# Two output tiles of group 0 computed by seven half products instead of four whole ones, and a new order of all operations, in an attention and feed-forward kernel

## The chip, the core and the metric

The kernel runs on one core of a Trainium2 chip. Five engines work side by side, each through its own list of instructions in order, and wait for one another through semaphores: PE (matrix products), DVE and POOL (vector work), ACT (activations) and SP, which here only issues transfers. The metric is the device time of one execution in microseconds (us), as the median of several runs. The profile is one further execution, recorded by the hardware profiler.

## The reference

Attention with a squared ReLU in place of softmax, followed by a feed-forward layer with a quick GELU:

```python
scores = scale * np.matmul(q, k.transpose(0, 1, 3, 2))     # q, k, v: 8 x 12 x 448 x 64
attn = np.maximum(scores, 0.0) ** 2 / S
attn_out = np.matmul(attn, v)
x = np.ascontiguousarray(attn_out.transpose(0, 2, 1, 3)).reshape(B * S, H * D)   # 3584 x 768
h = x @ w_in                                                # 768 x 2048
g = h * (1.0 / (1.0 + np.exp(-1.702 * h)))
return (g @ w_out).astype(np.float32)                       # 2048 x 768
```

## The kernel before

The work is cut into 24 attention units (8 batches, 3 units of four heads each) and 8 groups of tokens, of 6 x 64 = 384 tokens (even groups) and 8 x 64 = 512 tokens (odd groups). A group's feed-forward work can begin when the units of its batches have delivered their columns of the transposed x.

The kernel's whole order is one hand-held list of short words (`words`, from line 468 on). `do(word)` parses each word and issues its operation. So the order of the words is the order of the instructions on every engine, and also the order of the transfers on the queues of SP, POOL and ACT. The part after `@` gives the PSUM banks (0 to 7) that the operation takes; a new tile in a bank waits until the readers of the bank's last tile are done. The part after `:` names the engine (`a` ACT, `d` DVE, `p` POOL) where it isn't the usual one.

The words, with their lines in the profile:

| word | operation | engine |
|---|---|---|
| `Lk6`, `Lq6` | load k or q of unit 6 in float32 into the one staging buffer of k (`kst`) or q (`qst`) | SP's queue (L99) |
| `K6`, `Q6` | cast it to float16, which frees the staging buffer | ACT, POOL or DVE (L79, L83) |
| `Rk6`, `Rq6` | transpose it by a transfer | SP's queue |
| `jk1`, `jq1`, `V1` | load and cast k, q or v in one transfer; units 1 to 5 for k and q | POOL's queue (L104) |
| `tk1`, `ek1` | transpose on PE (L131) and its copy out; units 0 to 5 | PE, DVE |
| `s7.4@6.2` | scores of unit 7, part 4, into two banks | PE (L150) |
| `r7.4.1` | ReLU of one of the two banks | ACT (L163) or DVE (L161) |
| `x7.4` | square of both halves | DVE (L88), ACT (L169), POOL (L88) |
| `a7` | squared scores times v: 28 matmuls | PE (L181) |
| `e7.0.1` | copy of a part of the result into x of a group | ACT, DVE |
| `f0.3.1` | first product of the layer, plain: two matmuls of group 0 or 1 | PE (L228) |
| `u2.1.4` | first product by seven half products: product 4 of group 2, block 1; six matmuls | PE (L203, `hx`) |
| `S`, `T` | sums of w_in blocks and of x blocks that these need | DVE (L88) |
| `t`, `b`, `g`, `v` | snapshot, add, GELU and scaling to float16 of the first product | ACT, DVE, ACT, POOL (L79, L88, L214, L217) |
| `m0.1.0` | second product, plain: tile 1 of group 0, output half 0; 16 matmuls of 384 columns | PE (L203, `op`) |
| `n0.1.0` | its copy to the output tile | ACT, DVE |
| `p1.0.4` | second product of two tiles together by seven half products: product 4 for tiles 0 and 1 of group 1; 8 matmuls of 384 columns | PE (L203, `ox`) |
| `i2.2.1` | second product of one tile with the combined weights; 16 matmuls | PE (L203, `os`) |
| `A1.0.4` | sums of token tiles that `p` and `i` need (`asum` and in place) | DVE (L88) |
| `W2.4` | sums of w_out blocks: quarter 2 of combination 4 | DVE (L88, `wT`) |
| `h`, `l` | snapshot of a pair's bank to the output tile, and the final addition | ACT or DVE, DVE or ACT (L81, L85, L396) |
| `o`, `q` | store of a whole output tile (two transfers), or a half of a half tile | SP's queue; `q` also ACT's |
| `jwa`, `jwb`, `jo` | load of w_in pieces and w_out blocks | POOL's queue (L411, L415) |
| `G3` | a tiny transfer on SP that waits for the last w_in piece | SP's queue |

For two token tiles and the two output halves, four `m` of 16 matmuls are the plain way. The seven products (a Strassen form) take seven `p` of 8 matmuls. They accumulate in two banks, 0 for products 0, 2, 4, 5 and 1 for products 1, 3, 6. Between them the snapshots `h0`, `h2`, `h4` and the additions `l1`, `l3`, `l6` read the banks: product 2 waits for `h0`, 4 for `h2`, 5 for `h4`, 3 for `l1` and 6 for `l3`. Products 2 and 3 need the token sums `A.2` and `A.1` and weight combinations 2 and 1. Products 4 and 5 need `A.3` and combinations 3 and 4, and product 6 needs `A.4`.

Combination 3 overwrites a block of w_out in place:

```python
        o, x, y = {1: (t1, wout[1][0], wout[0][0]), 2: (t2, wout[1][1], t1),
                   3: (wout[1][0], wout[1][0], wout[1][1]), 4: (t4, wout[0][1], t2)}[n]
```

so all plain `m` of output half 1, which read the block as loaded, must come before the four `W.3`. In the kernel before, group 0's three tiles are the plain `m` and `n` (six `m`), and groups 1 to 7 use `p`, with `i` for the odd third tile of groups 2, 4 and 6.

The buffers that matter below: one each for `kst` and `qst`, two for the cast k and q, three for the transposed ones, four for v, five for `gf` (GELU results before scaling) and three output tiles.

Of the kernel before, what the change touches and what calls it, by code (L numbers as in the profile page):

```python
# [15 lines left out]
def kernel(  # L16
# [406 lines left out]
    with tc.manual_schedule():  # L423
# [35 lines left out]
        def zeros(e, p, n):  # L459
# [8 lines left out]
            "Lk0 z13@0 jk1 V1 jq1 I V0 K0:d tk0@1 z1 ek0 jk2 Lq0 Q0:a tq0@2 eq0 tk1@3 s0.3@4.5 "  # L468
            "r0.3.1 jq2 ek1 s0.1@6.7 r0.1.0 r0.3.0:d s0.0@0.1 s0.2@2.3 tq1@5 r0.0.1:d r0.2.0 "
            "s0.5@4.6 r0.1.1 s0.4@1.2 r0.0.0 r0.5.1 s0.6@7.0 eq1 r0.4.0:d tk2@5 x0.0 s1.0@1.6 "  # L470
            "r0.4.1 x0.4 jwb2 r0.5.0 x0.5 r0.6.1 jk3 r0.2.1 r0.6.0 x0.3:p jq3 x0.1 ek2 r1.0.1 "
            "r1.0.0 x0.2 x0.6 s1.5@2.4 s1.2@0.3 r1.2.0 s1.1@7.6 r1.1.1 tq2@5 a0@1.0 r1.1.0 r1.5.0 "
            "s1.6@6.7 eq2 r1.2.1 x1.0 r1.5.1 r1.6.0 s1.3@5.2 r1.3.0 x1.1 x1.2 tk3@3 e0.0.0 "
            "e0.0.1:a jk4 x1.5 e0.1.0:a tq3@4 r1.3.1 ek3 eq3 jwb0 x1.3 jq4 jwa0 s1.4@6.5 r1.6.1 "
            "V2 x1.6 r1.4.1 r1.4.0 s2.0@1.3 s2.2@2.7 r2.2.1 e0.1.1:a s2.1@4.5 r2.0.1 r2.0.0 "
            "r2.2.0 tk4@6 r2.1.1 x1.4 a1@7.0 e1.0.1:a ek4 r2.1.0:d x2.2 s2.6@3.6 r2.6.0 tq4@1 "
            "r2.6.1 e1.0.0 s2.3@2.4 r2.3.0 e1.1.1 x2.0 x2.1 eq4 s2.4@5.0 r2.3.1 jwa1 s2.5@3.6 "
            "f0.2.0@2 r2.4.0 r2.4.1 jwb1 jwa2 jq5 f0.3.0@4 s3.0@1.5 x2.6 e1.1.0 x2.3 f0.3.1 x2.4 "
            "jk5 r2.5.0 r2.5.1 x2.5 r3.0.0:d S0.1 V3 f0.2.1 f0.0.0@7 f0.0.1 s3.1@0.3 r3.0.1 "
# [24 lines left out]
            "b1.3.1 b1.2.3 g1.2.3 Rk7 u1.2.5 u1.2.6 u1.3.4 r6.1.0 W3.1 S0.4 v1.2 V7 u1.3.3 g1.2.5 "
            "v1.2.3 s6.4@4.5 s6.3@6.0 S1.3 n0.0.1 t1.3.4 g1.3.1 b1.2.6 b1.3.3 s6.5@3.7 r6.4.0 "
            "u1.3.5 x6.1:p r6.3.0:d r6.4.1:d r6.5.0 W1.2 v1.3.1 v1.2.5 u1.3.6 Lk8 g1.3.5 W3.2 V6 "
            "x6.4:a r6.3.1:d x6.2:a r6.5.1 Rq8 b1.3.6 K8:p m0.1.0@4 s6.6@6.3 W2.4 v1.3.5 g1.3.3 "
            "v1.3.3 s7.2@5.1 g1.2.6 x6.3 W1.4 v1.2.6 Lq9 g1.3.6 s7.0@0.2 r7.2.1 r7.0.0 x6.5:a Q9 "
            "r6.6.1:d r7.2.0:d Lk9 r7.0.1 m0.1.1@7 r6.6.0:d n0.1.0:a Rk8 s7.1@3.1 x6.6 W3.4 "
            "x7.0:a a6@5.0 s7.3@6.2 r7.1.0:d r7.1.1 n0.1.1 Lq10 s7.4@4.3 x7.2 e6.0.1:a K9:p "  # L510
            "r7.3.1 e6.1.1:a e6.0.0 r7.4.0:d p1.0.0@1 o0.0 r7.4.1:d e6.1.0:a s7.6@7.2 s7.5@0.5 "
            "r7.3.0 x7.1 x7.3 r7.6.0 r7.6.1:d r7.5.0 s8.2@4.6 m0.2.0@3 r7.5.1 r8.2.0:d V10 x7.4 "
            "s8.1@7.0 x7.6 r8.2.1 x7.5:a h1.0.0 n0.2.0:a s8.0@5.6 r8.1.1 a7@2.4 v1.3.6 r8.0.1 "
            "A1.0.1@0 A1.0.2@1 s8.3@3.0 W0.4 r8.3.0 r8.1.0:d e7.0.1 e7.1.1:a r8.3.1 p1.0.1@6 "
            "s8.5@7.3 V8 e7.0.0:a r8.0.0:d x8.1 e7.1.0 r8.5.0:d Rk9 r8.5.1 Rq9 s8.6@4.5 x8.0 x8.2 "
            "r8.6.1 x8.3:a p1.0.2 x8.5 r8.6.0:d s8.4@0.2 r8.4.1 s9.0@3.7 r8.4.0 l1.0.1 r9.0.0 "
            "x8.6 r9.0.1 x8.4 x9.0:a m0.2.1@5 n0.2.1:a s9.1@2.4 A1.0.4 r9.1.1:d Lk10 r9.1.0 "
            "a8@0.3 s9.2@7.5 e8.0.0:a Q10:d e8.0.1:a s9.3@4.2 r9.2.1:d r9.3.1 K10:p p1.0.3 "
            "u2.0.0@5 r9.2.0 Rk10 u2.1.0@2 Lk11 K11:p T2.1 W3.3 e8.1.0 T2.2 T2.3 e8.1.1:a "
            "s9.4@7.3 u2.0.1@0 W1.3 r9.4.1:d t2.0.0 u2.0.2 b2.0.1 t2.1.0 u2.1.2 u2.1.1@3 r9.3.0:d "  # L520
            "b2.1.1 W0.3 T2.4 r9.4.0 t2.0.2 u2.0.3 u2.0.4 g2.0.1 v2.0.1 t2.1.2 u2.2.0@7 g2.1.1 "
            "t2.0.4 b2.0.3 Lq11 t2.2.0 v2.1.1 u2.1.4 t2.1.4 h1.0.2 x9.2 u2.1.3 b2.1.3 u2.2.1@4 "
            "u2.0.6 g2.0.3 v2.0.3 b2.2.1 x9.4:a u2.2.2 u2.1.6 b2.0.6 g2.2.1 g2.0.6 Rq10 W2.3 "
            "u2.2.3 u2.3.0@0 Q11:a b2.1.6 t2.2.2:d u2.0.5 v2.0.6 g2.1.6 u2.3.1@3 g2.1.3 t2.3.0:d "
            "b2.3.1 v2.1.6 v2.2.1 u2.2.4 u2.1.5 u2.3.2 u2.3.3 t2.2.4 u2.2.5 A1.0.3 b2.2.3 u2.2.6 "
            "Lk12 o0.1 g2.3.1 t2.3.2 v2.3.1 v2.1.3 g2.0.5 g2.1.5 v2.0.5 u2.3.4 p1.0.4 g2.2.3 "
            "g2.2.5 s9.6@5.2 v2.1.5 b2.2.6 s9.5@4.7 t2.3.4:d u2.3.5 x9.1:a v2.2.3 K12 Lq12 b2.3.3 "
# [147 lines left out]
```

## Time and profile before

| what | value |
|---|---|
| median of 10 runs | 369.87 us |
| lowest, highest | 369.34, 371.35 us |
| the profiled execution, device time | 369.0 us |
| its span, first to last instruction | 367.2 us |
| granted clock of PE | 0.996 |
| ACT relu at L163 | 215 x 564 ns |
| DVE relu at L161 | 121 x 618 ns |
| ACT square at L169 | 57 x 956 ns |
| DVE square at L88 | 84 x 663 ns |
| POOL casts of k at L83 | 12 x 952 ns |
| HBM read, written | 45.61 MB, 11.01 MB |

The device time is 1.8 us more than the span of the profile. A mean duration of ACT or DVE includes the overlap with the next instruction; two relus of ACT in a row start 0.42 us apart. "Releaser" in a line is what ended the idle time before an instruction. The chain of waits is followed back from the last instruction, so a piece "DVE" in it means that PE's next work waited for DVE there.

The start and end of the execution frame it: PE's first matmul, a warming product of zeros, starts at 1.16 us and its last matmul starts after 360.99 us; the last instruction is a store.

### The profile page before, as it was taken

Reading aid. Unit: us, or ns where it says so; the run is one execution under the profiler, and the core shown is the slowest. Engines: PE = TensorE matmul, PEld = TensorE weight load, DVE = VectorE, ACT = ScalarE, POOL = GpSimd, SP = SyncE. Lnnn points to the kernel's source line nnn. Section 1 sums busy time; section 2 is a strip of 40 time slices with the busy share of each in tenths; the row PEclk is TensorE's granted clock in tenths of the full one; section 3 lists DMA queues with packets and bytes.
Section 4 is the critical chain, followed back from the end, with each engine's and each line's share of the span. In section 5 each row is a group of like instructions: output and inputs, shape, how many; then the busy total and the mean of one; then the engine's idle time right before and its main releaser. Section 6 shows DMA issues by size and latency. Waiting matters only on the chain.

```text
span 367.2 us, 9086 instructions
## 1 busy us (share of the span) xinstructions
PE 357.2 (97%) x3570; PEld 231.1 (63%) x3570; DVE 289.6 (79%) x519; ACT 276.9 (75%) x542; POOL 178.8 (49%) x229
## 2 busy tenths in 40 slices
PE   8899999999999999999999999999999999999994
PEld 4444545664579555885559755786549655787662
DVE  3999978599997877878898788767987899755642
ACT  3998976697879998889958998878985897274310
POOL 6838694675115585266404856367342536043300
PEclk9999999999999999999999999999999999999998
DMA  9999999789974785967573395367943042300244
GB/s 194 190 205 203 241 209 229 129 173 210 131 199 109 159 251 88 217 163 165 103 168 71 98 197 138 102 147 176 227 96 77 0 112 28 87 0 2 75 109 119
DMA packets 65227, 51.39 MB, mean 140 GB/s; under 512 B 35744, under 2 KB 61856, under 8 KB 65184
## 3 DMA queue, kind: packets, MB, share of 16 engines
q1 hardware_dynamic: 48256, 36.32, 40.8%
q0 software_dynamic: 16608, 14.09, 25.9%
q8 instruction: 28, 0.46, 0.5%
q10 hardware_dynamic: 320, 0.39, 0.4%
q14 instruction: 15, 0.12, 0.1%
HBM read 45.61 MB, written 11.01 MB: 154 GB/s over the span
## 4 chain that ended last, share of the span: by engine, by line
PE 85%; DVE 10%; issue 1%; POOL 1%; ACT 1%; POOLq 0%; DVEq 0%
PE hx L203 29%; PE ox L203 26%; PE sc L150 9%; PE ht L228 7%; PE av L181 7%; DVE at L88 4%; PE os L203 4%; PE op L203 3%; DVE at L161 2%; DVE wT L88 1%; PE zp L463 1%; ACT at L163 1%; DVE asum L88 1%; PE tr L131 1%; POOL ge L217 1%
## 5 line engine op out<-in xcount | busy, mean ns | idle before, releaser
L163 ACT ACTIVATE at<-sc 128x448 f16<-128x448 f32 x215 | 104.8, 564 | 13.3 <-PE sc L150 13.0
L161 DVE TENSOR_SCALAR at<-sc 128x448 f16<-128x448 f32 x121 | 71.8, 618 | 13.0 <-PE sc L150 12.5
L217 POOL TENSOR_SCALAR go<-gf 128x512 f16<-128x512 f32 x64 | 41.2, 644 | 63.8 <-ACT gf L214 47.0
L88 DVE TENSOR_TENSOR gf<-hx,gf 128x512 f32<-128x512 f32 (+1 forms) x78 | 47.9, 627 | 26.8 <-PE hx L203 14.2
L203 PEld LDWEIGHTS <-win 128*128 128x128 f16 x624 | 56.4, 98 | 8.4 <-issue 2.8
L88 POOL TENSOR_TENSOR at<-at 128x896 f16<-128x896 f16 x27 | 45.6, 1694 | 30.1 <-ACT at L163 18.5
L217 POOL TENSOR_SCALAR ge<-gf 128x384 f16<-128x384 f32 x64 | 35.8, 559 | 46.1 <-ACT gf L214 28.9
L169 ACT ACTIVATE at<-at 128x896 f16<-128x896 f16 x57 | 53.9, 956 | 0.9 <-DVE at L161 0.6
L88 DVE TENSOR_TENSOR at<-at 128x896 f16<-128x896 f16 x84 | 52.8, 663 | 0.8 <-ACT at L163 0.4
L150 PE MATMUL sc<-qT,kT 64*64 64x448 f16 x672 | 51.7, 359 | 1.7 <-DVE at L161 0.6
L214 ACT ACTIVATE gf<-gf 128x512 f32<-128x512 f32 (+1 forms) x78 | 43.3, 580 | 9.4 <-DVE gf L88 9.4
L203 PE MATMUL ox<-wout,go 128*128 128x384 f16 x256 | 46.5, 327 | 0.0
L203 PEld LDWEIGHTS <-winS 128*128 128x128 f16 x468 | 42.7, 98 | 4.5 <-issue 1.0
L203 PEld LDWEIGHTS <-go 128*128 128x128 f16 x320 | 29.9, 98 | 22.6 <-issue 4.8
L203 PEld LDWEIGHTS <-ge 128*128 128x128 f16 x288 | 27.5, 98 | 19.7 <-issue 3.3
L79 ACT ACTIVATE gf<-hx 128x512 f32<-128x512 f32 (+1 forms) x51 | 27.3, 543 | 15.3 <-PE hx L203 7.2
L203 PE MATMUL hx<-T,winS 128*128 128x256 f16 (+1 forms) x312 | 37.0, 260 | 0.0
L181 PE MATMUL av<-at,v 64*64 64x448 f16 x672 | 36.1, 350 | 0.1
L150 PEld LDWEIGHTS <-kT 64*64 64x64 f16 x672 | 17.4, 105 | 27.0 <-issue 22.2
L203 PE MATMUL hx<-xo,win 128*128 128x256 f16 x252 | 32.1, 273 | 0.0
L203 PE MATMUL ox<-wT,asum 128*128 128x384 f16 x176 | 31.8, 327 | 0.0
L203 PEld LDWEIGHTS <-asum 128*128 128x128 f16 x200 | 18.7, 98 | 15.3 <-issue 3.1
(78 smaller groups left out, 483.3 us busy)
## 6 DMA issues: line engine op xcount, KB each, us to landing
out_dram<-osb SPq DMA_DIRECT2D x52, 192.0 KB, 3.2
kst<-in_k_dram SPq DMA_DIRECT2D x19, 448.0 KB, 4.6
qst<-in_q_dram SPq DMA_DIRECT2D x19, 448.0 KB, 4.1
v<-in_v_dram POOLq DMA_DIRECT2D x24, 224.0 KB, 5.2
win<-in_moe_w_in_dram POOLq DMA_DIRECT2D x8, 384.0 KB, 9.7
wout<-in_moe_w_out_dram POOLq DMA_DIRECT2D x4, 768.0 KB, 12.3
k<-in_k_dram POOLq DMA_DIRECT2D x5, 224.0 KB, 6.2
q<-in_q_dram POOLq DMA_DIRECT2D x5, 224.0 KB, 6.2
```

The costliest lines, as they stand in the source:

```text
L79: nc.scalar.activation(out=o, in_=i, func=AF.Copy)
L88: eng[e].tensor_tensor(out=o, in0=x, in1=y, op=op)
L131: nc.tensor.matmul(out=ps[64 * a:64 * a + 64, j * 128:(j + 1) * 128], lhsT=x[:, a, 64 * j:64 * j + 64], rhs=ident[:, :], is_transpose=True)
L150: nc.tensor.matmul(out=sc[a][c, 0:S], lhsT=st["kT"][r, j, c], rhs=st["qT"][r, :, c], start=True, stop=True)
L161: nc.vector.tensor_scalar(out=o, in0=i, scalar1=0.0, scalar2=None, op0=ALU.max)
L163: nc.scalar.activation(out=o, in_=i, func=AF.Relu)
L169: nc.scalar.activation(out=at, in_=at, func=AF.Square)
L181: nc.tensor.matmul(out=av[s][64 * a:64 * a + 64, 0:S], lhsT=v16[r, a, 64 * j:64 * j + 64], rhs=at[r, a, :], start=(j == 0), stop=(j == J - 1))
L203: nc.tensor.matmul(out=o, lhsT=lhs(i), rhs=rhs(i), start=start and i == 0, stop=i == n - 1, skip_group_check=True)
L214: nc.scalar.activation(out=o, in_=i, func=AF.Gelu_apprx_sigmoid, scale=1.0 / SC)
L217: eng[e].tensor_scalar(out=o, in0=i, scalar1=SC, scalar2=1.0, op0=ALU.mult, op1=ALU.mult)
L228: nc.tensor.matmul(out=hp[g, f][:, 0:n], lhsT=w[:, i, fo:fo + 128], rhs=xts[g][:, i, 0:n], start=i == 0, stop=i == NK - 1)
```

## The change

The list of words is replaced as a whole. No function changes.

- For group 0, `m0.0.*` and `m0.1.*` with their four `n` go. In their place stand `p0.0.0` to `p0.0.6`, `A0.0.1` to `A0.0.4`, `h0.0.0`, `h0.0.2`, `h0.0.4` and `l0.0.1`, `l0.0.3`, `l0.0.5`, `l0.0.6`. The third tile's `m0.2.0` and `m0.2.1` become `i0.2.0` and `i0.2.1`, with `A0.2.5`.
- All 1939 words (now 1950) are ordered anew. Many keep their neighbours but change bank or engine: 13 ReLUs go from ACT to DVE; DVE has 13 squares less, ACT 9 and POOL 4 more; three query casts go from POOL to ACT; four `e` copies go from ACT to DVE.
- The sixteen `W` sums stand earlier; before, the four `W.3` stood behind `m0.2.1`.
- The loads and stores on the queues of POOL and SP are ordered anew as well.

The core of the difference, the opening, the place of group 0's output and the end:

```diff
-            "Lk0 z13@0 jk1 V1 jq1 I V0 K0:d tk0@1 z1 ek0 jk2 Lq0 Q0:a tq0@2 eq0 tk1@3 s0.3@4.5 "
...
-            "r0.4.1 x0.4 jwb2 r0.5.0 x0.5 r0.6.1 jk3 r0.2.1 r0.6.0 x0.3:p jq3 x0.1 ek2 r1.0.1 "
...
-            "u1.2.1@7 b1.2.1 g1.2.1 v1.2.1 v1.6 m0.0.0@5 u1.2.3 g1.2 s6.2@4.3 T1.3 Lq8 t1.3.0 "
-            "s6.1@6.2 u1.3.2 S0.3 t1.2.2 n0.0.0:a r6.2.0 u1.2.4 r6.1.1:d r6.2.1:d s6.0@5.4 r6.0.1 "
-            "r6.0.0 x6.0:a t1.3.2 V11 t1.2.4:d W0.1 u1.3.1@2 W2.2 Rq7 W0.2 m0.0.1@3 K7:p Q8:a "
...
-            "x6.4:a r6.3.1:d x6.2:a r6.5.1 Rq8 b1.3.6 K8:p m0.1.0@4 s6.6@6.3 W2.4 v1.3.5 g1.3.3 "
...
-            "r6.6.1:d r7.2.0:d Lk9 r7.0.1 m0.1.1@7 r6.6.0:d n0.1.0:a Rk8 s7.1@3.1 x6.6 W3.4 "
...
-            "q7.2.0.0:a p7.2.3 h7.2.2:d A7.2.4 p7.2.4 o7.1 p7.0.6 h7.2.4:d l7.2.3 l7.0.6 o7.0 "
-            "q7.3.1.1:a q7.2.0.1 q7.3.1.0:a p7.2.5 l7.2.5:a q7.3.0.0 q7.3.0.1 p7.2.6 l7.2.6 "
-            "q7.2.1.1:a q7.2.1.0"
+            "z13@0 Lk0 K0:d jq1 Lq0 jk1 I tk0@1 Q0:a z1 tq0@2 tq1@3 ek0 jwb2 eq0 s0.1@4.5 "
...
+            "f1.2.1 W3.2 v0.9 g1.1 v0.14 f1.4.1 f1.4.2 g1.0 f1.6.0@3 f1.6.1 v1.0 K7 u1.2.0@5 W1.1 "
+            "g1.4 t1.2.0 b1.2.1 v1.1 u1.3.0@2 f1.2.2 g1.2 f1.6.2 u1.2.2 v1.4 p0.0.0@1 t1.3.0 "
+            "t1.2.2 g1.6 W2.2 Rq6 s6.0@6.0 r6.0.1 T1.3 W0.1 s6.2@4.3 r6.2.0 W3.3 W3.4 A0.0.1@0 "
...
+            "A0.0.3 W0.3 W2.4 h0.0.0 p0.0.1@3 g1.2.5 r6.1.1 g1.3.1 v1.6 Rk7 V8 t1.3.2 g1.2.3 Lq7 "
+            "Q7:a u1.2.6 v1.2.3 u1.3.3 p0.0.2 u1.3.4 x6.1:p s6.3@0.5 b1.2.6 l0.0.1 h0.0.2 "
+            "r6.3.0:d v1.3.1 s6.5@4.7 r6.5.1:d t1.3.4 Rq8 b1.3.3 W0.4 p0.0.3 Lq9 V6 W1.4 r6.5.0 "
+            "r6.3.1 x6.3 x6.5:a s6.6@0.7 r6.6.0 A0.0.4 s6.4@4.5 r6.4.1:d r6.4.0 p0.0.4 r6.6.1 "
+            "u1.3.5 u1.3.6 g1.2.6 b1.3.6 x6.6:p h0.0.4 Rq7 x6.2:a p0.0.5 Lk9 s7.0@0.4 x6.4:p "
...
+            "p7.2.4 h7.2.4:d q7.2.0.0:a l7.2.3 A7.2.4 p7.0.6 l7.0.6 q7.3.1.1 q7.3.1.0 q7.2.0.1:a "
+            "p7.2.5 l7.2.5:a o7.0 q7.3.0.1 q7.3.0.0 p7.2.6 l7.2.6 q7.2.1.1 q7.2.1.0:a"
```

On POOL's queue the opening transfers were `jk1 V1 jq1 V0 jk2 jq2 jwb2 jk3 jq3 jk4 jwb0 jq4 jwa0 V2 jwa1`, with the square `x0.3` between `jk3` and `jq3`. They are now `jq1 jk1 jwb2 jk2 jq2 jq3 jk3 V0 jwb0 V1 jq4 jk4 jwa0 jwa2 V2`, with the square `x1.0` between `jk4` and `jwa0`.

## The prediction

> **What bounds the kernel now.** First view, the page's busy times and the chain that ended last.
>
> ```profile
> PE 357.2 (97%) x3570; PEld 231.1 (63%) x3570; DVE 289.6 (79%) x519; ACT 276.9 (75%) x542; POOL 178.8 (49%) x229
> ...
> PE 85%; DVE 10%; issue 1%; POOL 1%; ACT 1%; POOLq 0%; DVEq 0%
> ```
>
> PE carries most of the chain, so removed matmuls can count, but the busy 97% has modelled ends. I therefore took, tile by tile, the distance from a tile's first matmul to the next tile's first in the trace. The shortest distance of each kind is its price: `s` 0.19 us, `a` 1.32, `f` 0.325 (group of 384 columns) or 0.43, `u` 0.495 or 0.655, `p` 1.30, `m` and `i` 2.60, about 0.1 for each change between 64-row and 128-row work. The chain shows two of them:
>
> ```profile
> 71.96 2.60 PE op L203 x16
> ...
> 344.25 18.21 PE ox L203 x112
> ```
>
> 112 matmuls in 18.21 us are fourteen `p` of 1.30. All of before's PE work at these prices is 349.9 us, 348.6 of it ahead of the last tile. The first matmul starts at 1.16 and the last tile at 360.99, so PE lost 359.8 - 348.6 = 11.2 us waiting: 6.3 up to 30 us, 2.0 between 82 and 98 us, 0.9 at 182 and 227 us, the rest in pieces under 0.08. The stretches by window agree:
>
> ```profile
> 0.00:10.00 10.00, 8.36 (x94) 4.71 (x95) 4.17 (x9) 4.09 (x7) 7.02 (x15) 1.00 0.94 195
> 10.00:20.00 10.00, 8.17 (x136) 4.18 (x133) 10.00 (x19) 10.00 (x25) 8.39 (x11) 1.00 1.23 191
> 20.00:30.00 10.00, 9.32 (x132) 5.09 (x131) 10.00 (x21) 8.61 (x22) 3.33 (x5) 1.00 1.25 205
> ...
> 80.00:90.00 10.00, 9.33 (x87) 4.96 (x86) 9.96 (x16) 7.95 (x16) 7.08 (x9) 1.00 0.99 192
> ```
>
> (PE, PEld, DVE, ACT, POOL busy; granted clock 1.00; DMA share.) In the head DVE, ACT and the DMA engines are all full. At 80 to 90 DVE is, and the chain there says with what:
>
> ```profile
> 77.29 0.69 DVE gf L88
> 77.98 1.06 DVE at L161 x2
> 79.05 2.52 DVE wT L88 x2
> ```
>
> **The change, part by part.** *Products.* Four `m` (4 x 2.60 = 10.40) become seven `p` (9.10): -1.30 us. Tile 2's two `m` become two `i` of equal length. One change of row size fewer: -0.1. PE work goes from 349.9 to 348.6. Bounds: -1.4 if PE stays the limit, 0 if every gap is refilled by waits; nearest is the tail row above, where `p` follow each other without a gap, so -1.4.
>
> The Trainium skill, Perfetto Trace Analysis, Identifying the Most-Contended Engine, speaks against this term: it calls matmul busy time a poor measure and judges headroom by weight loads, which here are 63% busy. By that rule PE has room and the term would be 0, the whole sum +0.1 instead of -1.3. The distances, which contain the waits, decide for me.
>
> *Other engines.* Distances priced likewise: ACT relu 0.424, ACT square 0.84, DVE relu or square 0.53, DVE asum 0.60, wT 0.47, POOL square 1.63, POOL cast 1.0. Counts: 13 relus go from ACT to DVE; DVE's 84 squares become 71, ACT's 57 become 66, POOL's 27 become 31; three query casts go from POOL to ACT; five `A` sums, three `h` and four `l` are added, four `n` removed. Totals: ACT 260.4 to 261.1 us, DVE 264.9 to 273.2, POOL 181.7 to 185.3. Below PE's 348.6, so over the whole they lie beside matmuls; what matters is each stretch.
>
> *Head.* PE's waits are partly loads:
>
> ```profile
> 11.71 0.58 PE L131 MATMUL tr<-ident,k 128*64 128x128 f16 x14 [0.65 <-DMA k<-in_k_dram]
> ...
> 24.22 0.81 PE L228 MATMUL ht<-xe,win 128*128 128x384 f16 x4 [0.38 <-DMA win<-in_moe_w_in_dram]
> ```
>
> Landings come one after another, about 1.1 us per 448 KB and 2 per w_in piece. In both orders the same twelve k, q, v loads and three w_in pieces stand up to `jwa0`, which landed at 24.1, so the first `f` cannot start before. New on POOL's queue: `jk3`, `V0`, `jwb0`, `V1` and `jq4` are behind waits for transposes, and `jwa0`, `jwa2`, `V2` behind the square `x1.0`, which waits for the relus of unit 1 at about 16 us. POOL reaches `jwa0` near 18, with `V1`, `jq4` and `jk4` still queued ahead of it, so the DMA engines do not run dry. `a0` needs `V0`, now tenth in line instead of sixth, and comes at about 16.0 instead of 14.7. Walking ACT from its first relu at 8.5 us: 14 relus and one square put `r1.0.0` at 15.3. Onward by the same prices `a1` follows `x1.3`, last of DVE's row there, at 21.2 instead of 20.4, `s2.5` waits for `r2.3.1` until 24.05, the first `f` comes at 24.35 (24.22 before), and `a2` at 27.6, since `V2` now follows `jwa2` and two of unit 2's squares are on POOL; before, `a2` stood 0.5 earlier against PE's own sum. I take +0.3; -0.4 if loads alone set it, +1.5 if DVE, with 1.0 us more work ahead of `a3`, falls behind.
>
> *Group 0's outputs.* The combination weights `W` (sixteen sums) now all stand ahead of `p0.0.5`; before, eleven stood ahead of `a6` and the four `W.3` waited for `m0.2.1`, the last reader of the unchanged weights. DVE has 25.4 us between `a5` and `a6` instead of 21.8, beside 32.2 of PE work (31.6). From `a6` to `a8` it falls from 15.5 to 13.7 beside 14.6 of PE. Such a sum costs its 0.47, or more beside POOL:
>
> ```profile
> L88 DVE TENSOR_TENSOR wT<-wout,wT 128x768 f16<-128x768 f16 x8 | 6.5, 838 | 0.0
> L88 POOL TENSOR_TENSOR at<-at 128x896 f16<-128x896 f16 x27 | 45.6, 1694 | 30.1 <-ACT at L163 18.5 <-DVE at L161 10.5 <-ACT gf L79 0.3
> ```
>
> One took 1.81 (79.68) while POOL cast and loaded. Walked by the rows, the sums run between 64 and 75 us, early, where before DVE idled 3.1 us (62.9 to 65.8). `b1.2.6`, ready at 73.9, stands behind the last four, which end at 75.0 by the prices and some 1.3 later with two meetings with POOL; it then ends at 77.0, and `s6.5`, which needs its bank 7, is due at 76.6. So PE is late by some 0.4 to 0.5 there; by 0.2 at `s6.4`, whose bank 5 waits for `r6.3.1` on ACT (78.6 against 78.5); and I allow 0.4 for `a7` and `a8`, where before lost 1.0: 1.1 instead of 2.0, so -0.9; -2.0 if all waits go, +1.5 if each of these sums meets a POOL instruction.
>
> The Trainium skill, SBUF — State Buffer, Who interferes with whom, says that a DVE instruction with two SBUF inputs and a GpSimd one that reads SBUF exclude each other for a whole instruction. The rows of 838 against 550 ns agree. If each of the four added POOL squares held up such a sum for its 1.69 us, the estimate is +6.8, and the whole sum +5.5.
>
> *Queue SP.* `Lq7` moves behind `Lq8`, and one staging buffer makes it wait for `Q8`; `Q7` goes on ACT, in order.
>
> ```profile
> qst<-in_q_dram SPq DMA_DIRECT2D x19, 448.0 KB, 4.1
> ...
> qT<-q SPq DMA_TRANSPOSE x18, 4.2
> ```
>
> `Q8` ends near 71.6, `Lq7` lands at 75.8, where ACT arrives at 74.9: one us of ACT with `h0.0.2`, `t1.3.4`, `r6.5.0` behind it. `Rq7` then lands near 82 and `s7.0` is due at 83.0. Hidden, by 1 us; included above.
>
> *From unit 9 on.* Stretch by stretch the loads resemble before's, but `a10` to `a11` has 10.0 us of DVE for 9.9 of PE (7.3 for 9.5) and `a12` to `a14` has 16.1 ACT and 15.4 DVE for 16.7 (13.3 and 13.6 for 16.0, where PE lost 0.7). I take +0.8; -0.9 if no wait is left, +2.5 as in the rival below.
>
> *Tail.* PE's last eight tiles are alike. `p7.0.0` now follows only `i6.2.1` after `u7.1.5`, whose gelu and widen end about 0.2 late; SP issues five stores after `l7.0.6` instead of six, but `l7.0.6` comes 0.5 later: -0.3. Together -0.1 (-0.4 to +0.4).
>
> Sum: -1.4 + 0.3 - 0.9 + 0.8 - 0.1 = -1.3. The profiled execution took 369.0 us (span 367.2), so 367.7 and a span of 365.9. The median of the ten runs is 0.87 higher, 369.87; forecast 368.6.
>
> **Rivals.** *Evacuation becomes the bound in unit 10 and units 12 to 14 (slower).* From 77.3 to 89.5 DVE took 12.2 us for work priced at 9.3, a factor 1.31. With it `a12` to `a14` needs 20.2 us against PE's 16.7, a loss of 3.5; the same rule gives 1.8 for before, which lost 0.7, so I take 2.4, or +1.7, and 1.3 more in unit 10. It decides once the factor passes 1.09 there. For it: DVE +8.3 in all. Against: the u-stretch ahead has only 16.9 DVE for 25.3 PE. Time: 369.87 - 1.4 + 0.3 + 3.0 = 371.8.
>
> *The gain is given back.* New waits anywhere equal the 1.4: 369.9. For it: both orders lost time wherever attention outran DVE. Against: the 82 us waits had a cause that is now elsewhere.
>
> *More than forecast.* Group 0's and the later waits go as well: -1.4 - 2.0 = 366.5.
>
> *`Lq7` late.* Landing 5 us or more after issue, as some transposes did, `s7.0` slips by 1.5 to 2 with everything behind: 370.5 to 371. Decides from a `Q7` end of about 78 us.
>
> *The change doesn't do what it says:* counting tiles excludes it, 64 matmuls become 56.
>
> **How the numbers follow.** Forecast case 0.40 (own range 367.4 to 369.3, two hundredths of it within noise), more 0.12, given back 0.20, evacuation 0.22, `Lq7` 0.06 (0.04 slower). Taking 0.2% (0.74 us) as what a measurement tells from no change: faster 0.38 + 0.12 = 0.50, same 0.02 + 0.20 + 0.02 = 0.24, slower 0.26. The range runs from the case of all waits gone, 366.5, into the evacuation rival, 371.4.
>
> **What would show it.** Matmul records 3562. First `f` within 0.5 us of 24.3. PE in 80 to 90 at 9.6 or more, against 9.33. The chain free of wT around 80. If instead 160 to 185 shows PE below 9.5 in a window with relu or asum of DVE on the chain, the rival holds. `a2` later than 28.5, or ACT idle ahead of `Q7` for over 2 us, would make the forecast wrong too.

## The result, and the profile after

| | before | after |
|---|---|---|
| median, runs of the comparison | 369.79 us, 50 runs | 372.28 us, 15 runs |
| lowest to highest | 368.72 to 372.23 | 371.54 to 373.01 |
| profiled execution, its span | 369.0, 367.2 us | 372.56, 370.8 us |

The change makes the kernel slower: ratio 1.0063, 95% interval 1.0048 to 1.0078, some 2.3 us. The forecast was 368.6 us; the result also lies above the range's end of 371.4.

First the page of the changed kernel, its busy times and the chain that ended last:

```profile
PE 357.8 (97%) x3562; PEld 232.0 (63%) x3562; DVE 300.0 (81%) x531; ACT 279.8 (75%) x537; POOL 184.4 (50%) x230
...
PE 83%; DVE 4%; ACT 4%; DMA 3%; POOL 3%; issue 2%; SPq 0%; POOLq 0%; ACTq 0%; DVEq 0%
```

The matmuls fell from 3570 to 3562, as they should, yet PE is busy 0.6 us longer and the span has grown by 3.6 us. The stretches that were shown of before (columns: PE, PEld, DVE, ACT, POOL busy; granted clock; DMA share; GB/s):

```profile
0.00:10.00 10.00, 7.63 (x90) 4.11 (x90) 4.51 (x10) 4.13 (x7) 5.83 (x14) 1.00 0.93 191
10.00:20.00 10.00, 6.80 (x103) 3.46 (x104) 9.81 (x14) 9.30 (x19) 6.74 (x9) 1.00 1.22 186
20.00:30.00 10.00, 9.57 (x121) 5.47 (x120) 9.33 (x20) 8.59 (x20) 8.46 (x10) 0.83 1.25 205
80.00:90.00 10.00, 9.54 (x96) 5.16 (x96) 8.34 (x15) 9.96 (x20) 8.63 (x9) 1.00 1.02 174
```

From 10 to 20 us PE is busy 6.80 us (8.17 before), while DVE is 9.81 us busy with only 14 instructions (19 before): one of them must be long. From 20 to 30 us PE looks full, but at a granted clock of 0.83. At 80 to 90 us PE does gain, 9.54 against 9.33.

With the prediction's prices for PE's tiles (each distance to the next tile, less its price) the profile gives PE's waits by stretch, in us:

| profile | to 45 us | 45 to 100 | 100 to 140 | from 140 | sum |
|---|---|---|---|---|---|
| before | 6.5 | 2.4 | 0.3 | 2.1 | 11.2 |
| after | 9.6 | 1.9 | 1.3 | 3.2 | 16.0 |

PE's own work fell by 1.37 us (349.9 to 348.6), its waits rose by 4.8, and the tail after PE's last matmul grew by 0.2: together 3.6, the difference of the spans. 3.1 us of the waits arise in the opening. One profile of each kernel is a sample of one; the medians differ by 2.5 us. What the stretches are worth in the medians was therefore measured.

### The profile page after: what moved, and what is told of

Same layout as the page of the kernel before. It is cut to its first block, busy times and chain, and to the rows that moved or that the text cites. A ratio compares the mean times of both kernels' runs of the same rounds, so it can differ in the third digit from the quotient of the medians.

```text
span 370.8 us, 9040 instructions
## 1 busy us (share of the span) xinstructions
PE 357.8 (97%) x3562; PEld 232.0 (63%) x3562; DVE 300.0 (81%) x531; ACT 279.8 (75%) x537; POOL 184.4 (50%) x230
## 4 chain that ended last, share of the span: by engine, by line
PE 83%; DVE 4%; ACT 4%; DMA 3%; POOL 3%; issue 2%; SPq 0%; POOLq 0%; ACTq 0%; DVEq 0%
PE ox L203 27%; PE hx L203 24%; PE sc L150 9%; PE av L181 9%; PE ht L228 7%; PE os L203 5%; DVE at L88 2%; DMA v<-in_v_dram 2%; ACT at L163 2%; DMA qst<-in_q_dram 1%; POOL at L88 1%; POOL ge L217 1%; DVE at L161 1%; POOL go L217 1%; ACT q L79 1%
## 5 line engine op out<-in xcount | busy, mean ns | idle before, releaser
L163 ACT ACTIVATE at<-sc 128x448 f16<-128x448 f32 x202 | 100.4, 557 | 14.1 <-PE sc L150 12.5
L161 DVE TENSOR_SCALAR at<-sc 128x448 f16<-128x448 f32 x134 | 78.4, 618 | 9.8 <-PE sc L150 9.2
L217 POOL TENSOR_SCALAR go<-gf 128x512 f16<-128x512 f32 x64 | 42.7, 667 | 63.6 <-ACT gf L214 60.4
L88 POOL TENSOR_TENSOR at<-at 128x896 f16<-128x896 f16 x31 | 52.9, 1711 | 27.6 <-ACT at L163 15.3
L169 ACT ACTIVATE at<-at 128x896 f16<-128x896 f16 x66 | 62.7, 962 | 2.8 <-DVE at L161 2.3
L150 PE MATMUL sc<-qT,kT 64*64 64x448 f16 x672 | 53.1, 363 | 3.4 <-DVE kT L83 2.2
L88 DVE TENSOR_TENSOR at<-at 128x896 f16<-128x896 f16 x71 | 47.6, 697 | 2.5 <-ACT at L163 2.1
L79 ACT ACTIVATE gf<-hx 128x512 f32<-128x512 f32 (+1 forms) x49 | 26.7, 549 | 16.8 <-PE hx L203 11.4
L203 PEld LDWEIGHTS <-ge 128*128 128x128 f16 x256 | 24.1, 98 | 17.7 <-issue 4.0
L203 PE MATMUL ox<-wT,asum 128*128 128x384 f16 x192 | 34.9, 327 | 0.0
L203 PEld LDWEIGHTS <-asum 128*128 128x128 f16 x224 | 20.9, 98 | 16.6 <-issue 2.8
```

Of the source, the lines that this page charges most:

```text
L79: nc.scalar.activation(out=o, in_=i, func=AF.Copy)
L88: eng[e].tensor_tensor(out=o, in0=x, in1=y, op=op)
L150: nc.tensor.matmul(out=sc[a][c, 0:S], lhsT=st["kT"][r, j, c], rhs=st["qT"][r, :, c], start=True, stop=True)
L161: nc.vector.tensor_scalar(out=o, in0=i, scalar1=0.0, scalar2=None, op0=ALU.max)
L163: nc.scalar.activation(out=o, in_=i, func=AF.Relu)
L169: nc.scalar.activation(out=at, in_=at, func=AF.Square)
```

## Which stretch loses: hybrids of the two orders

Both orders are lists of words that keep the same dependencies. So the first words of one order, followed by all other words in the order of the other, make a valid kernel. At the joint a bank was renamed where the next tile found it taken. The cut shows as `|`:

```diff
 open_before    (before up to | , then changed)   ... s3.4@1.5 f0.0.2 v0.1 | s3.3@2.6 r3.3.1:d V5
 open45_before  (before up to | , then changed)   ... S1.1 g0.14 g0.7 | v0.3 v0.8 s5.4@6.7
 open50_before  (before up to | , then changed)   ... r5.5.0:d r5.6.0:d f0.13.1 | v0.8 S2.2 f1.5.0@2
 open_after     (changed up to | , then before)   ... f0.0.1 f0.0.2 g0.0 | jwb3 r3.1.0 G3
 late_before    (changed up to | , then before)   ... u2.0.2 b2.0.1 r9.4.0 | V10 Lk10 K10:p
 late_after     (before up to | , then changed)   ... p1.2.5 l1.2.6 e10.0.1:a | v2.3.5 v2.3.6 Rk13
 mid_after      (open45_before up to | , then before)   ... A1.2.4 l1.2.3 p1.2.6 | v2.3.3 x11.0:p
 group0_after   (open50_before up to | , then before)   ... u2.0.2 b2.0.1 r9.4.0 | V10 Lk10 K10:p
```

What was expected of them:

> The first 178 operations in the order of the kernel before (up to the scaling of group 0's tile 1, about 31 us), then everything else in the order of the changed kernel; group 0 by seven products. Theory: TensorE's extra waits in the opening (9.4 us against 6.3 in the profiles) are kept to the end, so this should be about 3 us faster than the changed kernel's 372.3, near 369.3; first matmul of the feed-forward layer near 24.2 us instead of 27.4. Rival: the opening's delay is taken up later, because later stretches have their own bound, and the loss is made after 100 us: then 371.5 to 372.5.

> The mirror image: the first 169 operations in the order of the changed kernel (to about 33 us), then everything else in the order of the kernel before, group 0's outputs by whole products. Theory: the opening's 3.1 us of waits stay, so near 372.9 (369.8 + 3.1). Rival (the loss is made after 100 us, where the changed order has 2.1 us more of waits): 369.8 to 370.5.

> As the first hybrid, but cut where both orders have done almost the same work (284 operations, about 45 us), because the earlier cut fell between loads of w_in pieces that the two orders take in different turns and cost 1.3 us at the seam. Theory (TensorE's waits add up by stretch; up to 45 us 9.6 us in the changed kernel's profile, 6.5 before): 3 us faster than the changed kernel, ratio to before 0.998 to 1.000. Rival (the opening's delay is taken up later): still 1.005.

> The kernel before up to 45 us, the changed order from there to about 140 us (it holds group 0's seven products), the kernel before from there on. Theory: products -1.4, waits in this stretch +0.5 (3.2 us against 2.7), no loss elsewhere: 0.9 us faster than before, ratio 0.9975. Rival (the products gain nothing because the waits take it back): 1.000.

> The kernel before up to about 140 us with group 0 by whole products, the changed order from there on. Theory: only the waits from 140 us on are added (3.2 us against 2.1): ratio 1.003. Rival (these waits are hidden, since later work has slack): 1.000.

> The kernel before up to its 314th operation (about 51 us), the changed order from there; cut where TensorE need not wait at the joint (the cuts at 31 and 45 us cost 1.3 and 2.4 us there). It is the changed kernel without its opening. Theory (the opening's waits are what the change loses): waits up to 60 us as before, 6.5 us against 9.7, ratio to before 1.000 to 1.001. Rival (later waits take up what the opening leaves): 1.004 or more.

> The kernel before up to 51 us, the changed order from there to about 107 us (only group 0's outputs and unit 6 to 8), the kernel before from there on. Theory: products -1.4 and the waits of 60 to 100 us 1.2 to 1.8 us instead of 2.3, nothing else changed: 1.4 to 2 us faster than before, ratio 0.995 to 0.997, so faster than both kernels. Rival (the products' gain is given back in waits): 1.000.

> The changed order up to about 107 us, the kernel before from there on: the changed kernel without its late part. Theory: the opening +3.2, products and group 0 -1.4 to -2, late waits as before: ratio 1.003 to 1.005, about 1 us faster than the changed kernel. Rival (the late part is where the time goes): 1.000.

Measured (the waits are those of one profile each, by the same prices):

| kernel | median us | ratio to before, interval | waits to 45 / 45 to 100 / 100 to 140 / from 140 | of these at the joint |
|---|---|---|---|---|
| open_before | 371.5 | 1.0052 (1.0025 to 1.0079) | 8.6 / 1.4 / 1.2 / 2.9 | 1.3 |
| open_after | 373.24 | 1.0092 (1.0067 to 1.0117) | 11.3 / 2.2 / 0.6 / 2.1 | 0.9 |
| open45_before | 373.4 | 1.0091 (1.0058 to 1.0124) | 8.9 / 3.7 / 1.3 / 3.2 | 2.4 |
| mid_after | 373.58 | 1.0093 (1.0058 to 1.0127) | 7.2 / 4.9 / 1.3 / 4.3 | 2.4 and 2.2 |
| late_after | 370.7 | 1.0033 (1.0009 to 1.0056) | 7.0 / 2.4 / 0.3 / 3.1 | none |
| open50_before | 370.54 | 1.0031 (1.0018 to 1.0043) | 7.0 / 2.1 / 1.3 / 3.6 | 0.8 |
| group0_after | 369.62 | 1.0009 (0.9984 to 1.0033) | 6.6 / 3.4 / 0.6 / 2.0 | 0.8 |
| late_before | 371.14 | 1.0056 (1.0039 to 1.0074) | 9.8 / 1.3 / 1.0 / 2.1 | 0.4 |

The first cuts were bad ones. In open_before the two orders load w_in pieces in different turns; in open45_before and mid_after, first cut at 45 us, two score tiles in a row want banks whose relus have not run. Those four say little, though open_after came out as expected and open_before on its rival. mid_after missed its expected ratio by 4.4 us, of which its joints make 4.6, and open45_before by at least 3.4, of which its joint makes 2.4.

The later ones agree in the main. late_before and group0_after, on one chip, differ only in what stands ahead of 51 us (and in the banks renamed there): 1.5 us. The changed kernel and open50_before differ in the same way: 1.2 us by the ratios. In both pairs the kernel without the changed opening bears the joint's 0.8 us alone (late_before has 0.4 at its own joint), so the opening itself may cost about 2 us. Without it open50_before is still 1.0031, over its expected 1.000 to 1.001, so the opening is not all. The order from 140 us on costs 1.2 us on top of before (late_after, as expected). The order from 107 us on costs 0.9 on top of group0_after (open50_before), but only 0.3 on top of late_before (1.0056, the whole changed kernel 1.0063), which was to gain about 1 us by leaving it out. The middle, which was to bring 2.3 us, brings nothing: group0_after misses its expected 0.995 to 0.997 and lands on its rival, "given back". Its joint makes 0.8 us of the miss. Against the forecast, the middle is the larger miss, 2.6 us; the opening's is 0.9 to 1.7.

## The opening: one square on POOL

The timeline of the changed kernel, all engines (columns: start, duration in us, engine, line, operation, out<-in, what it waited for):

```profile
15.75 0.58 PE L131 MATMUL tr<-ident,k 128*64 128x128 f16 x14 [0.72 <-DMA k<-in_k_dram]
15.87 0.62 DVE L83 COPY qT<-tr 128x896 f16<-128x896 f16 x1
...
16.03 0.71 POOL L104 DMA_DIRECT2D k<-in_k_dram  x1
16.40 3.23 DVE L88 TENSOR_TENSOR at<-at 128x896 f16<-128x896 f16 x1
16.73 0.70 POOL L411 DMA_DIRECT2D win<-in_moe_w_in_dram  x1
...
16.86 1.52 PE L181 MATMUL av<-at,v 64*64 64x448 f16 x28 [0.53 <-DMA v<-in_v_dram]
17.43 1.71 POOL L88 TENSOR_TENSOR at<-at 128x896 f16<-128x896 f16 x1
...
18.21 0.54 PE L150 MATMUL sc<-qT,kT 64*64 64x448 f16 x5
...
19.56 0.61 DVE L83 COPY kT<-tr 128x896 f16<-128x896 f16 x1
...
20.22 0.38 PE L150 MATMUL sc<-qT,kT 64*64 64x448 f16 x3 [1.48 <-DVE kT L83]
...
23.09 2.54 PE L181 MATMUL av<-at,v 64*64 64x448 f16 x28
```

The DVE square `x1.2` takes 3.23 us instead of 0.62, while POOL squares `x1.0` beside it. Behind it stands `ek3` (the copy to kT at 19.56), which frees a bank of `s1.4`, and PE waits 1.48 us in the middle of that tile. PE's granted clock is then 0.50 from 21.46 to 24.87 us, so that `a1` takes 2.54 us instead of 1.5. Ahead of it PE waited 0.72 us for `jk3` and 0.53 for V0: late loads have a part in this opening as well. Five profiles with the changed opening have the long row, at 3.22 to 3.26 us.

Five experiments turn on this stretch. Three move one word of the changed kernel, one moves the same square in the kernel before, one adds work for PE:

```diff
 square_dve
-"... e0.0.1 s1.6@3.0 jwa0 x1.0:p s1.4@7.2 ... x1.6 r2.1.0 x1.4 x1.3 e0.1.0:a ..."
+"... e0.0.1 s1.6@3.0 jwa0 s1.4@7.2 ... x1.6 r2.1.0 x1.4 x1.3 x1.0 e0.1.0:a ..."
 square_early
-"... x1.5:a eq2 x1.2 ek3 r1.3.1 e0.0.1 s1.6@3.0 jwa0 x1.0:p s1.4@7.2 ..."
+"... x1.5:a eq2 x1.0 x1.2 ek3 r1.3.1 e0.0.1 s1.6@3.0 jwa0 s1.4@7.2 ..."
 v_early
-"... s0.2@3.5 jk2 ... r1.1.0:d V0 jwb0 ..."
+"... s0.2@3.5 V0 jk2 ... r1.1.0:d jwb0 ..."
 square_pool (the kernel before)
-"... r1.2.1 x1.0 r1.5.1 ... s1.4@6.5 r1.6.1 V2 x1.6 ..."
+"... r1.2.1 r1.5.1 ... s1.4@6.5 r1.6.1 V2 x1.0:p x1.6 ..."
 keep_busy
-"... jwa0 x1.0:p s1.4@7.2 ..."
+"... jwa0 x1.0:p z10@7 s1.4@7.2 ..."
-                nc.tensor.matmul(out=zp[0][:, 0:NOUT], lhsT=zero[:, 0:128], rhs=zero,
+                nc.tensor.matmul(out=zp[-1][:, 0:NOUT], lhsT=zero[:, 0:128], rhs=zero,
```

> The changed kernel with one operation moved: the square x1.0 from POOL to DVE, behind x1.3. Theory: the square x1.2 on DVE took 3.23 us instead of 0.62 because a POOL instruction held it up; without the POOL square it ends near 17.0 instead of 19.6, the score tile behind it loses its 1.5 us wait, and the kernel is 1.3 to 2.0 us faster than the changed one, 370.3 to 371.0. Rival A: the POOL transfers issued at 16.0 and 16.7 us held it up, not the square; then x1.2 is still longer than 1.5 us and the gain is under 0.8. Rival B: the loads set the opening, x1.2's delay is beside the point: 372.3 and the first feed-forward matmul stays near 27.4 us.

> The changed kernel with one transfer moved: V0 ahead of jk2 on POOL's queue, where it lands at about 11.6 us instead of 16.8, and jk2 to jk3 each land 1.1 us later. Rival theory (V0 set the opening: a0 came at 16.9 us instead of 14.7): a0 near 15.2 and a kernel 1 us or more faster, near 371. Theory of the held-up square: a0 is only moved about among score tiles that wait for the same relus and casts, and unit 2's and 3's transposes come 1 us later, so 372.0 to 373.3.

> The kernel before with one operation moved: the square x1.0 from DVE to POOL, behind V2 on its queue, which is the place it has in the changed kernel (between two w_in loads). It doubles the suspected cost. Theory: a square of DVE beside it takes 1.5 to 3.2 us instead of 0.6, the casts ek3 and eq3 behind it come 1 us or more later, and the kernel is 0.5 to 1.5 us slower, ratio 1.0015 to 1.004. Rival (POOL's square does not hold up DVE; what held up x1.2 was its own input): all squares of DVE stay at 0.6 and the kernel is the same or 0.5 us faster.

> The changed kernel with the square x1.0 on DVE instead of POOL, ahead of x1.2. Theory: all DVE squares take 0.6 us, ek3 ends near 18.0 instead of 20.2, TensorE is not idle long enough to lose its clock, and the kernel is 1 to 2 us faster than after_again, ratio 1.001 to 1.004. Rival (the opening is set by loads and by DVE's amount of work, one square more eats the gain): equal to after_again.

> The changed kernel with ten products of zeros (about 1.6 us) into a free bank ahead of the score tile s1.4, which stands 1.5 to 1.9 us waiting for ek3; their result is overwritten. Theory: the wait itself stays, but the granted clock stays at 1.00 in 20 to 28 us (0.68 and 0.89 in the changed kernel), a1 takes 1.5 us instead of 2.5, and the kernel is 0.5 to 1.2 us faster than after_again. Rival (the halved clock costs nothing, since DVE sets this stretch): equal to it, or up to 1 us slower where the zeros come late.

> The changed kernel itself, as the direct comparison for the two above on the same chip: ratio 1.005 to 1.008.

| kernel | median us | ratio to before, interval |
|---|---|---|
| square_dve | 373.6 | 1.0091 (1.0061 to 1.0120) |
| v_early | 373.21 | 1.0087 (1.0054 to 1.0120) |
| square_pool | 373.6 | 1.0108 (1.0079 to 1.0137) |
| square_early | 370.77 | 1.0028 (1.0005 to 1.0050) |
| keep_busy | 372.45 | 1.0101 (1.0061 to 1.0140) |
| after_again | 372.42 | 1.0063 (1.0039 to 1.0086) |

square_pool is the clearest. One square moved from DVE to POOL makes the kernel before 1.08% slower, 4.0 us, more than was expected. First the kernel before, its DVE alone, then the timeline of square_pool:

```profile
15.14 0.61 DVE L83 COPY qT<-tr 128x896 f16<-128x896 f16 x1
15.67 1.68 DVE L88 TENSOR_TENSOR at<-at 128x896 f16<-128x896 f16 x3
17.27 0.55 DVE L83 CAST xe<-av 128x384 f16<-128x384 f32 x1
```

```profile
15.05 0.61 DVE L83 COPY qT<-tr 128x896 f16<-128x896 f16 x1
15.58 3.69 DVE L88 TENSOR_TENSOR at<-at 128x896 f16<-128x896 f16 x2
...
17.07 1.70 POOL L88 TENSOR_TENSOR at<-at 128x896 f16<-128x896 f16 x1
...
17.33 0.58 PE L131 MATMUL tr<-ident,k 128*64 128x128 f16 x14 [0.82 <-DMA k<-in_k_dram]
...
18.88 0.58 PE L131 MATMUL tr<-ident,q 128*64 128x128 f16 x14 [0.97 <-DMA q<-in_q_dram]
19.19 0.55 DVE L83 CAST xe<-av 128x384 f16<-128x384 f32 x1
```

Two squares that before took 0.53 us each, one after the other, take 3.69 together, and `e0.0.0` behind them starts at 19.19 instead of 17.27. From 16 to 20 us PE was busy 1.99 of 4 us (3.20 before), but part of that is not the square's: the waits named there are for `jk3` and `jq3`, which were issued 0.1 us earlier than before and landed 0.8 and 1.2 us later. Behind `x1.0` three w_in pieces were issued 1.6 us later as well; no wait of PE is named for them before the first `f` at 27.12. So the 4.0 us are shown for the move as a whole; how much of it is the held square, one profile doesn't say.

Taking the square off POOL brought the time back in one kernel of two. In both, the DVE squares of the opening are back at 0.6 us. square_early is 1.65 us faster than the changed kernel on the same chip (370.77 against 372.42), most of what the opening costs; by the ratios it is 1.3 us, and the intervals overlap. Its profile is of one of its longest runs (372.46): no square is held there, yet the first `f` comes at 27.53, since PE waited 1.57 us for `jk3` and 0.31 for V0. So late loads alone can cost what the held square costs. square_dve, which puts the square just ahead of `a1`, gained nothing in the median (expected 370.3 to 371.0), although its one profile, of its shortest run, was 1.1 us shorter than the changed kernel's, with the first `f` at 26.21. Why its other runs were longer is open.

V0's turn on the queue is not the cause: landing earlier (11.7 us instead of 16.8) made `a0` come later, at 19.1, since `jk3` then landed at 18.2 and PE stood 2.7 us ahead of `tk3`. That is more than the 1.1 us expected of the turn, and no gain. In its profile `x1.2` had started 1.7 us ahead of POOL's square and took 0.61 us: the same square on POOL held nothing up there.

The half clock is not the cause either. The stretches of the changed kernel and of keep_busy, in which PE multiplies zeros while it would wait:

```profile
16.00:20.00 4.00, 2.22 (x45) 1.13 (x41) 4.00 (x3) 3.30 (x6) 4.00 (x6) 1.00 1.25 204
20.00:24.00 4.00, 3.58 (x42) 1.90 (x45) 4.00 (x10) 3.12 (x8) 3.24 (x5) 0.68 1.25 205
24.00:28.00 4.00, 4.00 (x69) 2.72 (x59) 3.54 (x8) 3.46 (x10) 3.22 (x2) 0.89 1.25 205
```

```profile
16.00:20.00 4.00, 2.83 (x48) 1.52 (x43) 4.00 (x4) 3.83 (x8) 3.98 (x5) 1.00 1.23 197
20.00:24.00 4.00, 3.59 (x42) 1.65 (x40) 3.99 (x9) 2.69 (x8) 3.92 (x6) 1.00 1.24 200
24.00:28.00 4.00, 4.00 (x72) 2.54 (x69) 4.00 (x10) 3.93 (x10) 2.64 (x2) 1.00 1.25 204
```

The clock stays at 1.00 where it had fallen to 0.68 and 0.89, and yet the first `f` comes at 27.47 (27.41 in the changed kernel) and the median is the same, 372.45. Three of its seven runs took 374.45 to 376.25 us, which makes its ratio 1.0101; none shows a gain. DVE, full in five of these six rows, probably sets this stretch.

## Group 0: where the products' gain went

mid_plain takes the products away again, inside mid_after:

```diff
-"... p0.0.0@1 t1.3.0 t1.2.2 g1.6 W2.2 ... W3.3 W3.4 A0.0.1@0 ... p0.0.2 u1.3.4 ..."
+"... m0.0.1@1 t1.3.0 t1.2.2 g1.6 W2.2 ... W3.4 ... m0.1.1@1 W3.3 W2.3 W1.3 W0.3 u1.3.4 ..."
...
-"... r6.4.0 p0.0.4 r6.6.1 ... r7.4.1:d p0.0.6 r7.2.0 ..."
+"... r6.4.0 m0.0.0@3 r6.6.1 ... r7.4.1:d m0.1.0@3 r7.2.0 ..."
```

> mid_after with group 0's first two tiles by four whole products in the places of the first, third, fifth and seventh half product, without the token sums, and with the four sums of combination 3 behind the second of them. Theory (TensorE is the limit there): 1.3 us slower than mid_after, ratio 1.001. Rival (the evacuation is the limit; four sums and three copies less on DVE and ACT): equal to mid_after or faster.

It took 380.94 us, ratio 1.0303 (1.0252 to 1.0353), 7.4 us over mid_after. That is no measure of the products: the four sums of combination 3, now in a row behind `m0.1.1`, took 4.27 us beside a POOL square, and `b1.2.6` behind them made PE wait 3.2 us at 81 us. Inconclusive.

The profile of group0_after names three waits in this stretch: 0.8 us at 54 us (`a5` for `x5.6`, at the joint; a sum of w_in blocks ahead of it took 2.52 us beside a POOL square, 1.51 before) and these two, with nothing else above 0.2 up to 100 us:

```profile
74.90 0.81 PE L203 MATMUL hx<-T,winS 128*128 128x256 f16 x6 [0.76 <-DVE gf L88]
...
87.83 0.38 PE L181 MATMUL av<-at,v 64*64 64x448 f16 x4 [1.13 <-DMA v<-in_v_dram]
```

The first is `u1.3.3`, which waits for `b1.3.1`, queued on DVE behind sums of w_out blocks. The second is `a6`, for V6: the changed order loads V7, V8 and only then V6, issued at 79.9 and landed at 87.8. Both are in the changed kernel too (0.9 us at 76, 0.6 at 88). The mends:

```diff
 mended and mended_two
-"... f0.15.2 S2.4 f0.9.0@1 ... x5.6 a5@0.4 ..."
+"... f0.15.2 f0.9.0@1 ... x5.6 S2.4 a5@0.4 ..."
-V7 ... V8 ... V6
+V6 ... V7 ... V8
 mended alone
-"... b1.2.3 W0.2 W1.2 g1.2.1 W2.3 r6.1.0:d K8:p v1.2.1 b1.3.1 W1.3 ..."
+"... b1.2.3 b1.3.1 W0.2 W1.2 g1.2.1 W2.3 r6.1.0:d K8:p v1.2.1 W1.3 ..."
```

> group0_after with three moves: the sum S2.4 behind x5.6 (a5 waited 0.8 us for x5.6), the addition b1.3.1 ahead of four sums of w_out blocks (u1.3.3 waited 0.9 us for it), and V6 first of V6, V7, V8 on POOL's queue (a6 waited 1.3 us for V6, which landed at 87.8 us). Theory (the products' gain is there, and these three waits hide it): waits between 45 and 100 us fall from 3.4 to about 0.5 us, the kernel is 2 to 3 us faster than group0_after, ratio to before 0.992 to 0.996, faster than both kernels. Rival (DVE is full, each wait comes back elsewhere): 0.999 to 1.001.

> group0_after with two of the three moves: the sum S2.4 behind x5.6, and V6 first of V6, V7, V8 on POOL's queue; b1.3.1 stays behind the sums. Theory (the meeting of a sum with POOL's square x6.1 cost mended its 3.4 us; the other two moves gain what was expected): waits of 45 to 100 us 1.2 to 1.8 us instead of 3.4 in group0_after and 5.8 in mended, the kernel 1.5 to 2 us faster than group0_after, ratio 0.995 to 0.998. Rival (DVE is full between 60 and 90 us whatever the order; waits come back): 1.000 to 1.004.

| kernel | median us | ratio to before, interval | waits to 45 / 45 to 100 / 100 to 140 / from 140 |
|---|---|---|---|
| mended | 371.96 | 1.0054 (1.0032 to 1.0077) | 7.1 / 5.8 / 0.6 / 2.1 |
| mended_two | 368.29 | 0.9973 (0.9954 to 0.9993) | 6.6 / 2.1 / 0.6 / 2.0 |

mended missed, and its timeline shows the same thing as the opening:

```profile
76.43 2.00 POOL L88 TENSOR_TENSOR at<-at 128x896 f16<-128x896 f16 x1
...
76.81 2.03 DVE L88 TENSOR_TENSOR wout<-wout,wout 128x768 f16<-128x768 f16 x1
...
80.37 0.38 PE L150 MATMUL sc<-qT,kT 64*64 64x448 f16 x4 [3.25 <-DVE gf L88]
```

With `b1.3.1` moved ahead, a sum of w_out blocks met POOL's square `x6.1`, took 2.03 us instead of 0.54, and `b1.2.6` behind it made `s6.5` wait 3.25 us. Leaving that one move out leaves the meeting out. mended_two beats both kernels, by 0.27% and 0.9% of the ratios to before, as expected. Its lines:

```profile
PE 355.3 (97%) x3562; PEld 230.0 (63%) x3562; DVE 292.9 (80%) x522; ACT 279.5 (76%) x547; POOL 180.6 (49%) x229
...
PE 82%; DVE 11%; issue 2%; ACT 2%; POOL 1%; ACTq 0%; POOLq 0%
```

```profile
74.89 0.81 PE L203 MATMUL hx<-T,winS 128*128 128x256 f16 x6 [1.52 <-DVE gf L88]
...
86.52 1.49 PE L181 MATMUL av<-at,v 64*64 64x448 f16 x28
```

`a6` no longer waits. `u1.3.3` still does, for 1.5 us. PE's waits are 11.2 us as before the change, so the products' 1.37 us remains: the span is 366.0 against 367.2, and PE's last tile starts 1.26 us earlier. The profile is of one of the shorter runs, 367.74 us.

## Why the prediction was wrong

*Products, -1.4: right, as far as is shown.* PE's own work fell by 1.37 us, and mended_two, with the waits of before, is 1.0 us faster by its ratio (0.1% to 0.5% by the interval). No run takes the products alone away: mid_plain, which was to, is inconclusive. What the prediction drew from the Trainium skill (Perfetto Trace Analysis, Identifying the Most-Contended Engine), a term of 0 since weight loads keep PE busy for only 63%, did not come out in mended_two, where they are 63% too.

*Head, +0.3 (-0.4 to +1.5): this step failed.* The first `f` was to come at 24.35 and came at 27.41, `a2` at 27.6 and came at 30.28, past the 28.5 that the prediction itself had named as a sign of being wrong. In the medians the opening costs 1.2 to 1.7 us, about 2 with the joints counted. `jwa0` landed at 24.4 as walked, so this load did not set the first `f`. The walk priced every DVE square at 0.53 us and let the POOL square `x1.0` cost only the transfers queued behind it; beside it `x1.2` took 3.23. A smaller part is loads: `a0`, walked to 16.0, came at 16.86, waiting for V0. square_pool and square_early show what the move of the square costs, not how it divides between the hold and the loads.

The Trainium skill (SBUF — State Buffer, Who interferes with whom), whose rule the prediction weighed for the sums of group 0 alone, names this case: a DVE instruction with two SBUF inputs contends with a GpSimd one that reads SBUF. The rows agree in kind: 3.0 to 3.3 us instead of 0.6 in six profiles with POOL's square close behind, 0.6 in square_dve and square_early without. The page also says that the order of issue decides who waits. By the recorded starts DVE came first here and waited all the same, and POOL's recorded spans are rough, so the runs do not settle that part. A walk by mean durations (663 ns for DVE's squares) hides the whole effect.

*Group 0's outputs, -0.9 (-2.0 to +1.5): right sign in the trace, wrong places, and in the medians the larger miss.* Waits between 60 and 100 us fell from 2.3 to 1.8 us (forecast 1.1). The late addition named, `b1.2.6`, cost nothing here, `b1.3.1` cost 0.9, and V6 behind V7 and V8 on POOL's queue, 0.6, was not walked at all though every queue was to be. With products the middle was to give -2.3; group0_after gave +0.3 (-0.6 to +1.2), of which 0.8 is its joint. Two moves brought mended_two to -1.0: `S2.4` undoes the joint's wait, V6 one of the order's own. So waits held the gain back.

*Queue SP: right.* `Lq7` landed at 77.5, `Q7` ended at 79.4, later than walked like all else there, and `s7.0` did not wait; nor did it in group0_after, with before's opening.

*From unit 9 on, +0.8: right size.* From 107 us on the changed order cost 0.9 and 0.3 us in two pairs; late_after, from 140 us on alone, measured 1.2 (0.3 to 2.1). The places differ: the largest waits of the changed kernel are at 116 to 119 us, where a snapshot on DVE waits 1.37 us for POOL's widen to free one of the five `gf` buffers, 0.7 at 180 and 0.6 at 220. No run changed these places, so their causes are read from the trace alone.

```profile
117.49 1.68 POOL L217 TENSOR_SCALAR ge<-gf 128x384 f16<-128x384 f32 x3
...
118.02 0.56 DVE L83 COPY gf<-hx 128x384 f32<-128x384 f32 x1 [1.37 <-POOL ge L217]
```

*Tail, -0.1:* +0.2 in the profile.

*Rivals.* Evacuation as the bound in units 10 and 12 to 14 named the right total (371.8) by the wrong mechanism: from 160 to 180 us PE is full, 10.00 of 10 in both windows. Its price was also below its own rule: a factor of 1.31 on 10.0 us of DVE beside 9.9 of PE makes 3.2 us in unit 10, not 1.3. "More than forecast" did not come about. "Given back" is what happened in the middle of this order, and mended_two shows that it need not.

## What to carry to other kernels

Where an operation is put on POOL, look at what DVE does at that moment, not at POOL's row: a square of 1.7 us on POOL held nothing up in v_early, and putting it there cost square_pool 4 us. Walk every load that is renumbered on a queue to its first user, also those that only change turns among themselves. A chain of small waits can be located by hybrids of two orders, if the cut is where both have done nearly the same work; otherwise the joint costs as much as the effect.

## What the runs showed of the hardware

- The held DVE row starts up to a microsecond ahead of the recorded start of POOL's square (16.40 against 17.43; the second of the pair in square_pool, 0.53 after 15.58, against 17.07) and ends 0.4 to 0.5 us after it. While POOL only issued transfers, DVE's squares took 0.6 us (square_dve). The hold depends on what DVE does: in all nineteen profiles, 23 squares of DVE started within a square of POOL and took 1.25 us in the median, while 655 ReLUs of DVE, which read PSUM, did so and none took more than 0.63. POOL's recorded spans are rough, so which part of the hold falls ahead of the square is not settled.
- PE's granted clock halves although PE is never idle for long: 2.22 us busy of 4, with no single wait over 1.9 us, was followed by a clock of 0.50 for 3.4 us, which makes the 0.68 and 0.89 of the two windows of 4 us, 1.7 us of clock in all. 2.83 of 4 kept it at 1.00. No rule comes out of the runs: the clock halved after a wait of 1.57 us in square_early (1.78 of the last 3.4 us busy), and stayed at 1.00 through one of 2.15 us in mid_after (1.25 of 3.4). The Trainium skill (TensorE: Matmul & The Clock Gate, Part 1: The HAM clock gate) speaks of half rate after an idle window of about 3.4 us; here a partly busy one was enough. And in keep_busy a full clock gained nothing that could be measured.
- The same load order lands differently from run to run: `jk3` at 15.7 us in one profile of the changed kernel and 16.9 in another, with DVE's long square and the median unchanged. One profile of an opening is one sample.
